# Moving the matmul operands of a gated feed-forward kernel by multiples of 64 bytes in SBUF

## The chip, the cores and the metric

The kernel runs on one core of a Trainium2 chip. The metric is the device time of one execution in microseconds (us); the profile is of one execution and shows each engine: PE is TensorE's matmuls, PEld its weight loads, DVE is VectorE, ACT ScalarE, POOL GpSimd, SP the queue that issues the transfers.

## What is computed

A linear recurrence over 768 time steps with complex decay runs for 4 x 8 heads of width 48, and its output, seen as 3,072 tokens of width 384, goes through a gated feed-forward layer of width 1,536:

```python
new_re = ar * S_re - ai * S_im
new_im = ar * S_im + ai * S_re
S_re, S_im = (new_re + kv, new_im)
y[:, :, t] = np.einsum('bhd,bhde->bhe', q[:, :, t], S_re)
...
g = x @ w_gate
silu = g * (1.0 / (1.0 + np.exp(-g)))
val = x @ w_val
return (silu * val @ w_out).astype(np.float32)
```

## The kernel before

The recurrence is computed in chunks of 128 time steps. A chunk of one batch entry, all 8 heads, is a slab; there are 24. Its decays come from cumulative sums (two matmuls over the triangle `tri`, 384 columns wide, at L504) and functions on ScalarE; its scores and its output from small matmuls (L692, L758). Two slabs make a group g of 256 tokens, 12 groups in all.

The feed-forward layer runs per group in 12 steps of f, 128 of the 1,536 hidden columns each. `f1` (L941) multiplies the group's input, 256 tokens, with gate and value weights of that f: 2 x 3 blocks of 128 rows. For accuracy a number is split into a high and a low part (`xh`, `xl` for the input, `hh`, `hl` for the gated result, two halves of each weight tile), and a product is made of three matmuls: high with high, low with high, high with low. So f1 is 18 matmuls that load 128 columns of a `ww` tile and stream 256 columns of `xh` or `xl`. ScalarE and VectorE then make `sg`, `hh` and `hl`. `f2` (L980) is 9 matmuls that load 128 columns of a `wo` tile and stream 256 columns of `hh` or `hl`. In group 11 f2 is turned round (L974): it loads 128 columns of `hh` or `hl` and streams 384 columns of `wo`, six matmuls in each f step. Group 0 isn't split and runs in plain float32 while the weights arrive.

The order of all work on the engines is worked out ahead by a planner from costs and due times; f1 and f2 of consecutive steps, and the slabs' matmuls of later groups, are interleaved on TensorE by it.

Where a tile lies: `quick` opens the pool `const` and then the pool `work`. Every tile of `work` has a size per partition that is a multiple of 512 bytes: a `ww` tile has 6,144 bytes (`place("w", ...)`), a `wo` tile 3,072, a stage tile 3,072, and each `xh`, `xl`, `hh` and `hl` has its own size plus `TURN_OVER`, 128 numbers or 512 bytes. So all tiles of `work` begin at one address modulo 512. Called 0 here, it is that of both kinds of weights. Inside their larger tiles, x (`xh`, `xl`) begins `INPUT` and h (`hh`, `hl`) begins `GATED` numbers later, both 48, which is 192 bytes:

```python
ahead = GATED if tag in ("hh", "hl") else INPUT
t = work.tile([P, n + TURN_OVER], dt, name=tag, tag=tag, bufs=slots[tag])[:, ahead:ahead + n]
```

`tri` is the first tile of `const`; the sizes behind it add up so that it begins at 384. The blocks of 128 or 256 columns that one matmul reads are multiples of 512 bytes apart, so every read of a tile begins at its tile's offset. The last weight tiles (f = 9 to 11) are lent as buffers to the first stage and later hold the source of the gathers into `T` (L659).

Of the kernel before, what the change touches and what calls it, by code (L numbers as in the profile page):

```python
# [9 lines left out]
F32 = mybir.dt.float32  # L10
# [9 lines left out]
P = 128  # L20
# [37 lines left out]
WIDE_KEYS = 64  # L58
TURNS = P // WIDE_KEYS

TURN_OVER, GATED, INPUT = 128, 48, 48
HIGH, LOW, WHOLE = 0, 1, 2
SHY = -9.7365
POOL_FROM = 9.8301
# [169 lines left out]
def quick(ctx, tc, q, k, v, a_re, a_im, w_gate, w_val, w_out, out, count):  # L234

    nc = tc.nc
    PS = bass.MemoryType.PSUM
    const = ctx.enter_context(tc.tile_pool(name="const", bufs=1))
    work = ctx.enter_context(tc.tile_pool(name="work", bufs=1))
    dram = ctx.enter_context(tc.tile_pool(name="dram", bufs=4, space=bass.MemoryType.DRAM))  # L240
    psum = ctx.enter_context(tc.tile_pool(name="psum", bufs=1, space=PS))
# [16 lines left out]
    G = const.tile([96, B, H, 64], F32, name="G")  # L258
    vts = [const.tile([P, H, 64], F32, name=f"vt{i}") for i in range(2)]
    turned_v = [const.tile([P, 2, 2, 64], F32, name=f"vr{i}") for i in range(2)]  # L260
    W, HALVES = {}, {}
    WIDE = {"w": 2 * DM, "o": DM}

    def place(nm, f, dtype):
        return work.tile([P, 2 * WIDE[nm]], dtype, name=f"w{nm}{f}", tag=f"w{nm}{f}", bufs=1)

    def spare(nm):

        if nm not in W:
            W.pop((nm, NF - 1, WHOLE))  # L270
            W[nm] = place(nm, NF - 1, F32)
        return W[nm]
# [35 lines left out]
    for t, (nm, f, i) in {"re": ("w", 0, 0), "im": ("w", 0, 1), "s1": ("o", 0, 0), "s2": ("w", 1, 0), "s3": ("w", 1, 1),  # L308
                          "qt": ("o", 1, 0), "kt": ("o", 2, 0), "qs": ("w", 2, 0)}.items():
        n, nm_f = 96 if t == "qs" else D, (nm, NF - 3 + f)  # L310
        if nm_f not in W:
            W[nm_f] = place(*nm_f, F32)
        at = W[nm_f][:, i * A2:i * A2 + 2 * H * n].rearrange("p (h d) -> p h d", d=n)
        for j in range(2):
            fixed["lent", t, j] = at[:, H * j:H * j + H], nm_f
# [498 lines left out]
    def weight_ops(f):  # L814
        for nm, n, user in (("w", 2 * DM, "f1"), ("o", DM, "f2")):
# [5 lines left out]
            for i, w in enumerate((w_out,) if nm == "o" else (w_gate, w_val)):  # L821
                def ld(e, i=i, w=w, raw=raw, nm=nm):
                    if i == 0:
                        W.pop((nm, f), None)
                        W[nm, f, WHOLE] = place(nm, f, U32)
                        raw["all"] = W[nm, f, WHOLE].rearrange("p (n t) -> p n t", t=2)
                        raw["low"], raw["high"] = (raw["all"][:, :, x] for x in range(2))
                    o = raw["all"]
                    o = o if nm == "o" else o[:, i * DM:i * DM + DM].rearrange("p (k n) t -> p k n t", k=KT)
                    nc.sync.dma_start(out=o, in_=words(w, nm, f))  # L830
                loads.append(pl.add(f"wl{i}{N}", {"SP": 0.55}, ld, alloc=[] if i else lent, deps=list(loads), lat=1.4, move=1.09))
# [380 lines left out]
@with_exitstack  # L1212
def tile_kernel(ctx, tc, q, k, v, a_re, a_im, w_gate, w_val, w_out, out):
    nc = tc.nc
    w_gate, w_val, w_out = (w if w.dtype == U32 else w.bitcast(U32) for w in (w_gate, w_val, w_out))
    keep = ctx.enter_context(tc.tile_pool(name="keep", bufs=1))

    count = keep.tile([1, 32], I32, name="count")[:, 0:1]
    quick(tc, q, k, v, a_re, a_im, w_gate, w_val, w_out, out, count)
    fit = nc.values_load(count, min_val=0, max_val=P)  # L1220
    with tc.If(fit < P):
        general(tc, q, k, v, a_re, a_im, w_gate, w_val, w_out, out)
# [30 lines left out]
```

## Time and profile before

| | |
|---|---|
| time, median of 3 runs | 639.09 us (635.09 to 642.51) |
| the profiled execution | 636.64 us, its span 634.9 us |
| TensorE busy | 599.6 us, 94% of the span |
| VectorE, ScalarE busy | 504.4 us, 403.5 us |
| matmuls, weight loads | 7,050 each |

The span runs from the first to the last instruction of the profiled execution. A matmul's duration in the profile is longer than the time from its start to the next one's, since matmuls are pipelined; how fast TensorE goes is read from the starts.

### The profile page before, as it was taken

Reading aid. Unit: us, or ns where it says so; the run is one execution under the profiler, and the core shown is the slowest. Engines: PE = TensorE matmul, PEld = TensorE weight load, DVE = VectorE, ACT = ScalarE, POOL = GpSimd, SP = SyncE. Lnnn points to the kernel's source line nnn. Section 1 sums busy time; section 2 is a strip of 40 time slices with the busy share of each in tenths; the row PEclk is TensorE's granted clock in tenths of the full one; section 3 lists DMA queues with packets and bytes.
Section 4 is the critical chain, followed back from the end, with each engine's and each line's share of the span. In section 5 each row is a group of like instructions: output and inputs, shape, how many; then the busy total and the mean of one; then the engine's idle time right before and its main releaser. Section 6 shows DMA issues by size and latency. Waiting matters only on the chain.

```text
span 634.9 us, 17155 instructions
## 1 busy us (share of the span) xinstructions
PE 599.6 (94%) x7050; PEld 564.9 (89%) x7050; DVE 504.4 (79%) x932; ACT 403.5 (64%) x653; POOL 4.2 (1%) x15
## 2 busy tenths in 40 slices
PE   2689999989999999999989999999999999999995
PEld 1477778979989999999989999999999999999995
DVE  8999999999988968878969868769879868544432
ACT  7854548886695785957876975956966863211210
POOL 2000000000000000000000000000000000000000
PEclk9999999999999999999999999999999999999998
DMA  8899701244644654565466464554564642441200
GB/s 256 229 278 270 255 26 38 58 125 117 137 128 116 159 130 105 131 139 133 106 130 154 101 151 115 130 139 112 141 140 124 152 106 62 114 97 51 51 1 29
DMA packets 164218, 79.96 MB, mean 126 GB/s; under 512 B 127387, under 2 KB 159901, under 8 KB 164134
## 3 DMA queue, kind: packets, MB, share of 16 engines
q1 hardware_dynamic: 164134, 78.80, 48.7%
q8 instruction: 57, 0.93, 0.7%
q14 instruction: 27, 0.22, 0.1%
HBM read 59.83 MB, written 4.78 MB: 102 GB/s over the span
## 4 chain that ended last, share of the span: by engine, by line
PE 65%; DVE 13%; DMA 7%; ACT 6%; SPq 4%; issue 3%; DVEq 0%; ACTq 0%
PE p_gv L941 34%; PE p_po L980 13%; PE p_py L692 5%; PE p_ps L692 4%; ACT L1084 4%; PE p_po L974 3%; SPq L659 2%; PE p_pm L504 2%; PE p_pm L758 2%; DMA wo<-in_moe_w_val_dram 2%; DMA re<-in_a_re_dram 2%; ACT s L408 1%; DMA ww<-in_moe_w_val_dram 1%; DVE sg L952 1%; DMA T<-ww 1%
## 5 line engine op out<-in xcount | busy, mean ns | idle before, releaser
L941 PE MATMUL p_gv<-xh,ww 128*128 128x256 f32 x1596 | 305.2, 289 | 5.4 <-DVE sg L952 4.5
L941 PEld LDWEIGHTS p_gv<-xh,ww 128*128 128x128 f32 x1596 | 256.5, 189 | 14.0 <-DVE sg L952 6.7
L941 PE MATMUL p_gv<-xl,ww 128*128 128x256 f32 x726 | 201.6, 278 | 0.0
L1084 ACT ACT_TABLE_LOAD x119 | 152.7, 1283 | 2.1
L941 PEld LDWEIGHTS p_gv<-xl,ww 128*128 128x128 f32 x726 | 136.5, 188 | 0.1
L947 ACT ACTIVATE sg<-p_gv 128x256 f32<-128x256 f32 x144 | 54.6, 384 | 118.2 <-PE p_gv L941 112.9
L980 PE MATMUL p_po<-hh,wo 128*128 128x256 f32 x660 | 119.8, 279 | 0.0
L980 PEld LDWEIGHTS p_po<-hh,wo 128*128 128x128 f32 x660 | 100.7, 188 | 1.8 <-issue 1.8
L952 DVE TENSOR_TENSOR sg<-sg,p_gv 128x256 f32<-128x256 f32 x144 | 58.7, 412 | 52.6 <-ACT sg L947 52.5
L980 PE MATMUL p_po<-hl,wo 128*128 128x256 f32 x330 | 91.7, 278 | 0.0
L980 PEld LDWEIGHTS p_po<-hl,wo 128*128 128x128 f32 x330 | 62.2, 188 | 0.0
L353 DVE TENSOR_TENSOR hl<-sg,hh 128x256 fp32r<-128x256 f32 x132 | 54.6, 417 | 4.9 <-ACT hh L357 0.4
L408 ACT ACTIVATE s<-s 128x768 f32<-128x768 f32 x44 | 36.8, 844 | 12.5 <-DMA fr<-s 6.5
L692 PEld LDWEIGHTS p_ps<-T 96*64 96x64 f32 x768 | 35.8, 138 | 4.1 <-ACT T L357 1.2
L692 PE MATMUL p_ps<-T 96*64 96x128 f32 (+1 forms) x768 | 39.4, 254 | 0.0
L720 DVE TENSOR_TENSOR sc<-p_ps,turn 128x512 f32<-128x512 f32 x48 | 32.2, 687 | 5.2 <-PE p_ps L692 4.9
L357 ACT CAST hh<-sg 128x256 fp32r<-128x256 f32 x51 | 20.3, 402 | 22.7 <-DVE sg L952 15.5
L778 ACT CAST xh<-p_py 128x384 fp32r<-128x384 f32 x22 | 10.6, 480 | 31.0 <-PE p_py L692 30.9
L892 DVE TENSOR_REDUCE flags<-wo 128x1 f32<-128x384 f32 x36 | 19.6, 544 | 11.9 <-DMA wo<-in_moe_w_val_dram 8.6
L897 ACT ACTIVATE wo<-wo 128x384 f32<-128x384 f32 x36 | 19.9, 554 | 12.9 <-DMA wo<-in_moe_w_val_dram 11.6
L359 DVE CAST hh<-sg 128x256 fp32r<-128x256 f32 x81 | 23.1, 290 | 5.7 <-PE p_po L980 2.3
L692 PE MATMUL p_py<-sc,vr 128*32 128x128 f32 x384 | 26.1, 273 | 0.0
(149 smaller groups left out, 895.2 us busy)
## 6 DMA issues: line engine op xcount, KB each, us to landing
T<-ww SPq DMA_DIRECT2D x216, 64.0 KB, 2.5
wo<-in_moe_w_out_dram SPq DMA_DIRECT2D x24, 384.0 KB, 6.0
ww<-in_moe_w_gate_dram SPq DMA_DIRECT2D x12, 384.0 KB
ww<-in_moe_w_val_dram SPq DMA_DIRECT2D x12, 384.0 KB, 6.7
vt<-in_v_dram SPq DMA_DIRECT2D x24, 192.0 KB, 3.2
wo<-in_moe_w_gate_dram SPq DMA_DIRECT2D x12, 384.0 KB, 3.7
wo<-in_moe_w_val_dram SPq DMA_DIRECT2D x12, 384.0 KB, 4.2
re<-in_a_re_dram SPq DMA_DIRECT2D x11, 384.0 KB
```

The source lines that it names most:

```text
L353: V[e].tensor_tensor(out=out, in0=a, in1=b, op=op)
L357: nc.scalar.copy(out=out, in_=in_)
L359: nc.vector.tensor_copy(out=out, in_=in_)
L408: nc.scalar.activation(out=of(dst), in_=of(source), func=func, scale=scale, **kw)
L692: nc.tensor.matmul(out=o, lhsT=l, rhs=r, start=opens, stop=closes, tile_position=(0, width * slot), skip_group_check=True)
L720: nc.vector.tensor_tensor(out=s.rearrange("p (r m) t -> p r m t", m=2), in0=scores[qd].rearrange("p (r m) t -> p r m t", m=2), in1=m, op=A ...
L897: nc.scalar.activation(out=high(0), in_=high(1), func=AF.Square, accum_out=flags[:, fl_hi + j:fl_hi + j + 1])
L941: nc.tensor.matmul(out=gv[:, i, :], lhsT=l, rhs=r, start=(m == 0), stop=(m == len(mm) - 1))
L947: nc.scalar.activation(out=new("sg", I), in_=at_["gv", I][:, 0:2 * P], func=AF.Silu)
L952: nc.vector.tensor_tensor(out=sg, in0=sg, in1=at_["gv", I][:, 2 * P:4 * P], op=ALU.mult)
L980: nc.tensor.matmul(out=po[:, 2 * P * k:2 * P * k + 2 * P], lhsT=l[:, k, :], rhs=r, start=f == 0 and j == 0 and k != 1, stop=f == NF - 1 an ...
L1084: nc.scalar.preload_act_table_set(op.load)
```

## The change

Three offsets change, and the gate and value weights get a pool of their own between `const` and `work`. That pool begins with an empty tile of `STILL`, 112 numbers or 448 bytes; a third pool closes it with 64 empty bytes, so that `work` again begins at the address modulo 512 that it had. Modulo 512 and behind the output weights `wo` at 0, the weights `ww` then lie at 448 (before: 0), x at 128 (before: 192) and h at 64 (before: 192).

```diff
-TURN_OVER, GATED, INPUT = 128, 48, 48
+TURN_OVER, STILL, GATED, INPUT = 128, 112, 16, 32
@@
     const = ctx.enter_context(tc.tile_pool(name="const", bufs=1))
+    still = ctx.enter_context(tc.tile_pool(name="still", bufs=1))
+    gap = ctx.enter_context(tc.tile_pool(name="gap", bufs=1))
     work = ctx.enter_context(tc.tile_pool(name="work", bufs=1))
@@
+    still.tile([P, STILL], F32, name="ahead")
+    gap.tile([P, TURN_OVER - STILL], F32, name="behind")
@@
     def place(nm, f, dtype):
-        return work.tile([P, 2 * WIDE[nm]], dtype, name=f"w{nm}{f}", tag=f"w{nm}{f}", bufs=1)
+
+        pool = still if nm == "w" else work
+        return pool.tile([P, 2 * WIDE[nm]], dtype, name=f"w{nm}{f}", tag=f"w{nm}{f}", bufs=1)
```

## Rows read from the trace of the kernel before

**Rows 1.** The page, parts 1 and 2: engines' busy us, granted clock in 40 slices
```profile
PE 599.6 (94%) x7050; PEld 564.9 (89%) x7050; DVE 504.4 (79%) x932; ACT 403.5 (64%) x653; POOL 4.2 (1%) x15
...
PEclk9999999999999999999999999999999999999998
```

**Rows 2.** The page, part 4: chain that ended last, by engine, by line
```profile
PE 65%; DVE 13%; DMA 7%; ACT 6%; SPq 4%; issue 3%; DVEq 0%; ACTq 0%
PE p_gv L941 34%; PE p_po L980 13%; PE p_py L692 5%; PE p_ps L692 4%; ACT L1084 4%; PE p_po L974 3%; SPq L659 2%; PE p_pm L504 2%; PE p_pm L758 2%; DMA wo<-in_moe_w_val_dram 2%; DMA re<-in_a_re_dram 2%; ACT s L408 1%; DMA ww<-in_moe_w_val_dram 1%; DVE sg L952 1%; DMA T<-ww 1%
```

**Rows 3.** TensorE's waits, 250 to 625 us: engine, line, releaser: total, times, longest
```profile
PE p_pm L504 <- DVE G L353: 1.9, 1, 1.9
PE p_gv L941 <- DVE sg L952: 1.1, 1, 1.1
```

**Rows 4.** Timeline, TensorE from 253.98 us: start, us, engine, line, operation, operands, count
```profile
253.98 0.28 PE L941 MATMUL p_gv<-xl,ww 128*128 128x256 f32 x1
253.98 0.30 PEld L941 LDWEIGHTS p_gv<-xh,ww 128*128 128x128 f32 x2
```

**Rows 5.** Timeline of matmuls: first and last start of one stretch
```profile
253.30 0.28 PE L941 MATMUL p_gv<-xl,ww 128*128 128x256 f32 x1
...
276.42 0.28 PE L941 MATMUL p_gv<-xl,ww 128*128 128x256 f32 x1
```

**Rows 6.** Sums of two windows: length, matmuls' busy us and count, clock, DMA share, GB/s
```profile
253.30:276.50 23.20, 23.20 (x206) 1.00 0.49 116
530.00:553.20 23.20, 23.20 (x200) 1.00 0.40 93
```

**Rows 7.** Timeline of matmuls: first and last start of the other stretch
```profile
530.08 0.28 PE L941 MATMUL p_gv<-xl,ww 128*128 128x256 f32 x1
...
553.17 0.40 PE L941 MATMUL p_gv<-xh,ww 128*128 128x256 f32 x2
```

**Rows 8.** By line, six stretches between 217 and 625 us: count, busy us, mean ns
```profile
L941 PE MATMUL p_gv<-xl,ww 128*128 128x256 f32 x24 | 6.7, 281 | 0.0
L941 PE MATMUL p_gv<-xl,ww 128*128 128x256 f32 x6 | 1.7, 281 | 0.0
L941 PE MATMUL p_gv<-xl,ww 128*128 128x256 f32 x18 | 5.1, 281 | 0.0
L941 PE MATMUL p_gv<-xl,ww 128*128 128x256 f32 x12 | 3.4, 281 | 0.0
L941 PE MATMUL p_gv<-xl,ww 128*128 128x256 f32 x126 | 35.4, 281 | 0.0
L941 PE MATMUL p_gv<-xl,ww 128*128 128x256 f32 x55 | 15.5, 281 | 0.0
```

**Rows 9.** The same by line: 230 to 321 us, and the page's whole span
```profile
L941 PE MATMUL p_gv<-xl,ww 128*128 128x256 f32 x126 | 34.8, 276 | 0.0
...
L941 PE MATMUL p_gv<-xl,ww 128*128 128x256 f32 x726 | 201.6, 278 | 0.0
```

**Rows 10.** Timeline: first of two sums over tri, and the matmul behind them
```profile
285.08 0.34 PE L504 MATMUL p_pm<-s,tri 128*128 128x384 f32 x1
...
285.43 0.28 PE L941 MATMUL p_gv<-xh,ww 128*128 128x256 f32 x1
```

**Rows 11.** Timeline, group 11: fourth and last wide matmul of f2, and the next
```profile
596.33 0.34 PE L974 MATMUL p_po<-wo-1_336,hl 128*128 128x384 f32 x1
...
596.85 0.34 PE L974 MATMUL p_po<-wo-1_336,hl 128*128 128x384 f32 x1
597.03 0.28 PE L941 MATMUL p_gv<-xh,ww 128*128 128x256 f32 x1
```

**Rows 12.** Tile T and its gathers, 250 to 625 us: who waited for it: us, times
```profile
  DVE ww L650: 2.5, 3
  DVE sc L720: 2.3, 2
  DVE G L353: 1.6, 3
```

## Prediction

> **What bounds the kernel now.** I read the page first. TensorE is the bound: it shows 599.6 us busy in a span of 634.9 us, at the full granted clock until the last slice, so at its 2.4 GHz level throughout [rows 1]. The chain that ended last is 65% TensorE, and its two largest lines are L941 (the matmuls into p_gv, "f1") and L980 (those into p_po, "f2") [rows 2]. Then the waits: from 250 to 625 us TensorE waits 3.0 us in all for another engine [rows 3]. There the time is a count of matmuls times their step, the time from the start of one to the start of the next, and a change in the step reaches the end undiminished.
>
> The count follows from the loops. Groups 1 to 11 run 12 steps of f of 18 matmuls in f1, 11 x 12 x 18 = 2,376. Groups 1 to 10 run 9 in f2, 10 x 12 x 9 = 1,080. Together there are 3,456 matmuls that stream 256 columns, each with a load of 128 columns. The load for the next one runs beside the stream of the present one: the load issued at 253.98 lies under the matmul of 253.98 [rows 4]. So at every moment two reads of SBUF are under way, and their addresses are what the change moves.
>
> Now the step. In one undisturbed stretch 206 matmuls show in a window of 23.20 us [rows 6]; one of them began before 253.30, so 205 start between 253.30 and 276.42 [rows 5], 204 steps in 23.12 us: 113.3 ns. In another stretch of the same length 200 show [rows 6]; three began before it, so 197 start between 530.08 and 553.17 [rows 7], 196 steps in 23.09 us: 117.8 ns. The same instructions, shapes and distances run at two levels, which I call the short and the long step. They differ by 4.45 ns. The mean duration of a matmul tells them apart too, 281 ns in a long stretch [rows 8] and 276 ns in a short one [rows 9].
>
> How much runs long: by the matmuls that read xl, the long stretches hold 24 + 6 + 18 + 12 + 126 + 55 = 241 [rows 8] of 726 [rows 9], a third. A third of 3,456 is about 1,150 matmuls, and 1,150 x 4.45 ns = 5.1 us are paid now for the long step. Everything else, some 2,310 matmuls, runs short.
>
> **The change part by part.** It removes and adds no instruction, no transfer and no wait; the order is the same. It adds two tiles that nobody touches. What moves is where tiles begin, modulo 512 bytes. Call distance the start of the streamed tile minus that of the tile loaded beside it, modulo 512. Before, x and h lie at 192 and both kinds of weights at 0, so all 27 pairs of an f step have distance 192. After:
> - f1 with f1 (17 pairs of 27): 128 - 448 = 192 modulo 512, as before.
> - the last of f1 with the first load of f2 (1 pair): 128 - 0 = 128.
> - f2 with f2 (8 pairs): 64 - 0 = 64.
> - the last of f2 with the first load of f1 (1 pair): 64 - 448 = 128.
>
> So nothing moves within f1; f2 and the two seams do.
>
> What the distance is worth, the trace shows only on 384-wide matmuls. At distance 320 (group 11 streams wo and loads hh) three steps take 0.52 us, 173 ns each, and the seam behind them at distance 0 takes 0.18 us [rows 11]. Two steps at 128 and 0 (the sums over tri) take 0.35 us, 175 ns each [rows 10]. At the short step's rate per column 384 columns would take 170 ns. So the rows give 3 to 10 ns of stall for a wide matmul at other distances. That is the bound from above for f2 at 64: up to 10 ns on 1,080 matmuls, 10.8 us, less the 1.6 us that f2's third of long steps costs already, so +9.2 us. The bound from below is the short step everywhere in f2, 1,080 x 0.33 x 4.45 ns = 1.6 us gained; below that nothing, since no row has a shorter step than 113 ns. I take the row with most repeats, 320: 173.3 x 256/384 = 115.5 ns, 2.2 ns over the short step, 2.4 us on 1,080 matmuls.
>
> What it does to f1 is the larger half. The long step is a lasting pattern: it starts at a restart of TensorE and runs to the next one, over whole groups (126 xl matmuls of one stretch) [rows 8]. With one distance for all 27 pairs nothing on the way disturbs it. After the change each f step passes through 10 pairs at 64 and 128, so the two reads meet in another phase four times in 3.1 us. I expect that the long pattern doesn't hold through that and f1 falls back to the short step, which is the commoner one. That takes off the 5.1 us.
>
> **A rule that speaks against it.** These rows show steps that differ by distance and by stretch, with TensorE waiting for nobody [rows 3, 10, 11]. The Trainium skill, "TensorE: Matmul & The Clock Gate", Part 2, says that TensorE has two independent SBUF read ports and that loading the next weights takes no read bandwidth from the running matmul. By that rule addresses can't matter and the sum would be 636.6 us, unchanged; the two levels of one loop in the trace don't agree with it, though they don't prove that addresses are the cause.
>
> The rest is small. Group 11's 72 wide matmuls go from 320 to 448; with a stall of 0 to 10 ns in place of today's 3 that is -0.2 to +0.5 us. The 42 sums over tri meet other distances, a few ns each, under 0.3 us. The gate weights' tiles are also where the gathers into T start; from 250 to 625 us only VectorE waited for them, 6.4 us in all, and TensorE never [rows 12], so 64 bytes more or less there cost nothing as long as that holds. ScalarE and VectorE write x and h at other offsets, with the same sizes; where they wait on TensorE, that is hidden.
>
> Sum, on the profiled execution's own time: 636.64 - 5.1 + 2.4 = 633.9, call it 634. That execution stands 2.5 us under the median of 639.09; the three runs spread over 7.4 us, which is what 1,670 matmuls passing from one step to the other would make, so part of that spread may be the share of long steps.
>
> **The rivals.**
> 1. Nothing changes: the share of long steps is drawn at each restart as now. For it: 55 xl matmuls in the last stretch keep the long step although every f step there has six wide matmuls at another distance between them [rows 8, 11]. Against it: the wide rows differ by distance. Time 636.6, between 635 and 642.5 as the runs shown. Chance 0.30.
> 2. The other side: the pairs at 64 and 128 push every step into the long pattern. For it: the wide seam at distance 0 stalls most [rows 11] and the last 120 us are long already. Against it: after the sums over tri, at 128 and 0, the short step comes back [rows 9, 10]. Price 2,310 x 4.45 ns = 10.3 us, 646.9. It decides by itself once 9 matmuls of 10 run long. Chance 0.17.
> 3. f2 alone pays the upper bound, with f1 as now: 636.64 + 9.2 = 645.8. From 114.8 ns on f2's step outweighs what it saves, and at 123 ns the kernel is 1% slower. For it: 64 lies between 0 and 128, the distances of the worse rows. Chance 0.11.
>
> **How the numbers follow.** The forecast, f1 short throughout and f2 between 113.3 and 117.8 ns, has 0.42 and its own range is 631.5 (636.64 - 5.1) to 636.3 (f2 all long, + 4.8). The range that holds 8 in 10 takes in rival 1 and the lower parts of 2 and 3: 630 to 646. One per cent, about what a measurement here can tell from no change, is 632.7 and 645.5 about the median. Below 632.7 lies somewhat more than half of the forecast's chance, counting in a step shorter than any row has: 0.25. Above 645.5 lie most of rival 2 and half of rival 3: 0.20. The rest is 0.55.
>
> **What would show it.** Right: xl matmuls last 276 ns in the mean from 505 to 625 us too, and 205 starts fit in 23.1 us there; f2's step is near 115. Rival 1: stretches of 281 and 276 ns still alternate. Rival 2: 281 ns everywhere. Rival 3: f2's step near 123 ns with f1 mixed. A step below 113 ns anywhere would make my lower bound wrong.

## The result: slower by 0.6%, with the forecast's main step reversed

| | before | after |
|---|---|---|
| time, median of 19 runs each | 638.29 us (635.09 to 642.51) | 642.12 us (639.11 to 645.98) |
| ratio after to before | | 1.0061, 95% interval 1.0044 to 1.0078 |
| the profiled execution, its span | 636.64 us, 634.9 us | 640.98 us, 639.2 us |

The time lies inside the range of 630 to 646 and within 1% of before, but it moved the other way: 3.8 us up between the medians, where the forecast had 2.6 us down from the profiled execution.

The page after, of which I show TensorE's and the other engines' busy us (part 1), the granted clock (part 2), the chain of waits (part 4) and four groups of matmuls (part 5: count, busy us, mean ns):

```profile
PE 606.2 (95%) x7050; PEld 573.0 (90%) x7050; DVE 504.6 (79%) x932; ACT 404.1 (63%) x653; POOL 4.2 (1%) x15
...
PEclk9689999999999999999999999999999999999998
...
PE 75%; DVE 11%; DMA 4%; ACT 4%; SPq 4%; issue 2%; DVEq 0%
...
L947 PE MATMUL p_gv<-xh,ww 128*128 128x256 f32 x1596 | 310.0, 291 | 6.1 <-ACT xh L784 3.3
...
L947 PE MATMUL p_gv<-xl,ww 128*128 128x256 f32 x726 | 202.9, 279 | 0.0
...
L986 PE MATMUL p_po<-hh,wo 128*128 128x256 f32 x660 | 122.2, 281 | 0.0
...
L986 PE MATMUL p_po<-hl,wo 128*128 128x256 f32 x330 | 92.1, 279 | 0.0
```

Lines are 6 higher than before: L947 is f1, L986 is f2, L980 the turned f2 of group 11. Against [rows 1, 2] the counts are the same to the instruction, VectorE and ScalarE are the same within 0.6 us, and TensorE has 6.6 us more in its matmuls (8.1 us in its weight loads, which run beside them). Its share of the chain rose from 65 to 75%. The xl matmuls' mean went from 278 ns [rows 9] to 279.

TensorE's waits from 250 to 625 us, as [rows 3] (total, times, longest):

```profile
PE p_pm L510 <- DVE G L359: 0.5, 1, 0.5
PE p_gv L947 <- DVE sg L958: 0.2, 1, 0.2
```

The same two waits, 0.7 us in place of 3.0. Over all from 100 us on, the waits sum to 5.7 us after and 9.3 before. I read this as a slower TensorE that reaches VectorE's results later and waits less for them; then of what TensorE lost, 3.6 us came back at its own waits.

**Where the time went.** I sort the steps of 256-wide matmuls from 100 us on by the pair they pass through (start to start, breaks left out), and give the mean. These means, like the counts of stretches further down, are of one profiled execution of each kernel. xx is f1, hh is f2, xh the seam into f2, hx the seam back into f1:

| pair | distance before, after | recorded steps after | ns before | ns after | difference |
|---|---|---|---|---|---|
| xx | 192, 192 | 2,230 | 114.81 | 116.48 | +3.7 us |
| hh | 192, 64 | 951 | 114.61 | 117.68 | +2.9 us |
| xh | 192, 128 | 91 | 114.67 | 120.01 | +0.5 us |
| hx | 192, 128 | 80 | 114.81 | 115.91 | +0.1 us |

Some 7.2 us more on TensorE, 3.6 us of it back at the waits; beside that f1 of group 1 starts 1.7 us later (102.6 against 100.9 us), in a profile whose granted clock shows 6 and 8 tenths in its second and third slice, so partly the 1.2 GHz level, after a first slice with TensorE 2 tenths busy (before's first slice is as idle, and its clock did not fall). These terms give 5.3 us for the 4.3 us between the spans; the 1.0 us left I have not followed. The early clock is not what sets the two kernels apart: the granted clock averaged 0.992 over the 19 runs of after, and 0.992 over the 62 runs of before that stand beside the experiments below.

The largest term is the one that I had with the other sign: f1, whose own distance did not move. The timeline of matmuls (start us, duration, line, operands, count) shows it happen behind a restart:

```profile
256.30 0.28 PE L947 MATMUL p_gv<-xl,ww 128*128 128x256 f32 x1
...
257.32 0.28 PE L947 MATMUL p_gv<-xl,ww 128*128 128x256 f32 x1
257.44 0.28 PE L947 MATMUL p_gv<-xh,ww 128*128 128x256 f32 x1
257.56 0.40 PE L986 MATMUL p_po<-hh,wo 128*128 128x256 f32 x2
257.79 0.28 PE L986 MATMUL p_po<-hl,wo 128*128 128x256 f32 x1
...
258.50 0.28 PE L986 MATMUL p_po<-hl,wo 128*128 128x256 f32 x1
258.61 0.28 PE L947 MATMUL p_gv<-xh,ww-1_292 128*128 128x256 f32 x1
258.73 0.28 PE L947 MATMUL p_gv<-xl,ww-1_292 128*128 128x256 f32 x1
...
260.50 0.28 PE L947 MATMUL p_gv<-xl,ww-1_292 128*128 128x256 f32 x1
```

Every third matmul reads xl. Before the first f2 there are 9 steps in 257.32 - 256.30 = 1.02 us, 113.3 ns: short. In f2 6 steps take 0.71 us, 118 ns. And in the next f1, the same instructions at the same distance, 15 steps take 1.77 us, 118.0 ns: long. A window of 23.20 us from the restart on holds 199 matmuls, near the 200 of the long window of before and not the 206 of the short one (columns as in [rows 6]):

```profile
255.60:278.80 23.20, 23.20 (x199) 1.00 0.47 116
```

To count this over the whole trace I call a stretch a row of 256-wide matmuls of one line without a break, and long when the steps of its second half average 115 ns or more. Behind a restart means behind a break or behind other matmuls, the sums over tri and group 11's wide f2 among them:

| stretch | before: long of all | after: long of all |
|---|---|---|
| f1 behind a restart | 16 of 51 | 17 of 49 |
| f1 behind f2 | 27 of 78 | 72 of 80 |
| f2 behind f1 | 28 of 89 | 91 of 91 |

A restart gives f1 what it gave it before. The way through f2 and back turns it long.

### The profile page after: what moved, and what is told of

Its sections match the earlier page's. It is cut to its first block, busy times and chain, and to the rows that moved or that the text cites. A ratio compares the mean times of both kernels' runs of the same rounds, so it can differ in the third digit from the quotient of the medians.

```text
span 639.2 us, 17155 instructions
## 1 busy us (share of the span) xinstructions
PE 606.2 (95%) x7050; PEld 573.0 (90%) x7050; DVE 504.6 (79%) x932; ACT 404.1 (63%) x653; POOL 4.2 (1%) x15
## 4 chain that ended last, share of the span: by engine, by line
PE 75%; DVE 11%; DMA 4%; ACT 4%; SPq 4%; issue 2%; DVEq 0%
PE p_gv L947 39%; PE p_po L986 16%; PE p_py L698 5%; PE p_ps L698 5%; PE p_po L980 4%; SPq L665 2%; PE p_pm L510 2%; PE p_pm L764 2%; ACT L1090 1%; DMA wo<-in_moe_w_val_dram 1%; DMA T<-ww 1%; ACT s L414 1%; DMA dr<-qs 1%; DVE ww L359 1%; PE p_gv L636 1%
## 5 line engine op out<-in xcount | busy, mean ns | idle before, releaser
L947 PE MATMUL p_gv<-xh,ww 128*128 128x256 f32 x1596 | 310.0, 291 | 6.1 <-ACT xh L784 3.3
L947 PEld LDWEIGHTS p_gv<-xh,ww 128*128 128x128 f32 x1596 | 259.1, 190 | 14.7 <-DVE sg L958 4.4
L947 PE MATMUL p_gv<-xl,ww 128*128 128x256 f32 x726 | 202.9, 279 | 0.0
L947 PEld LDWEIGHTS p_gv<-xl,ww 128*128 128x128 f32 x726 | 136.5, 188 | 0.1
L986 PE MATMUL p_po<-hh,wo 128*128 128x256 f32 x660 | 122.2, 281 | 0.0
L986 PEld LDWEIGHTS p_po<-hh,wo 128*128 128x128 f32 x660 | 101.6, 188 | 1.8 <-issue 1.8
L986 PE MATMUL p_po<-hl,wo 128*128 128x256 f32 x330 | 92.1, 279 | 0.0
L986 PEld LDWEIGHTS p_po<-hl,wo 128*128 128x128 f32 x330 | 62.0, 188 | 0.0
```

Of the source, the lines that this page charges most:

```text
L947: nc.tensor.matmul(out=gv[:, i, :], lhsT=l, rhs=r, start=(m == 0), stop=(m == len(mm) - 1))
L986: nc.tensor.matmul(out=po[:, 2 * P * k:2 * P * k + 2 * P], lhsT=l[:, k, :], rhs=r, start=f == 0 and j == 0 and k != 1, stop=f == NF - 1 an ...
```

## The experiments

### The bare stream: step against distance

The slab work and all data flow are left out and zeros are written: only blocks of 36 matmuls that load 128 and stream 256 columns at one distance, with a break of TensorE between blocks (four blocks a distance), then a run of 128 f steps with the distances of four layouts.

```diff
+UNIFORM = [0, 32, 64, 96, 128, 160, 192, 224, 256, 288, 320, 352, 384, 416, 448, 480]
+PATTERNS = [(0, 0, 192, 192), (448, 0, 128, 64), (0, 0, 192, 64), (448, 0, 128, 192)]
```

> A bare stream that leaves the whole computation out and writes zeros: 36 matmuls of the kernel's form (load 128 columns, stream 256, fp32r) per block, one distance between streamed and loaded tile per block, 16 distances in steps of 32 bytes, 4 blocks each after a short idle; then 8 f steps of 18 and 9 matmuls with the four address sets before, after, f2 alone, seams alone. Theory pair (each pair costs what its own distance costs): distance 192 gives steps of 113.3 or 117.8 ns, 64 gives 117.7 or more in every block, 128 gives 118 to 120, 0 the most; in the pattern of after the 17 pairs of f1 stay at 113.3 or 117.8 as the restart drew them. Theory phase (a step depends on what the pairs before it did to the alignment of the two reads): the uniform blocks look alike at every distance, two levels each, and only patterns that change the distance on the way are long throughout. In both, the pattern of after averages about 116.9 ns, that of before between 113.3 and 117.8.

Measured, as the mean step from the 13th of a block on:

| distance | ns | distance | ns |
|---|---|---|---|
| 0, 256 | 120.0 | 128, 384 | 118.5 to 120.0 |
| 32, 288 | 116.5 to 117.8 | 160, 416 | 117.2 to 118.5 |
| 64, 320 | 117.7 to 117.8 | 192, 448 | 113.3 in three blocks, 117.7 to 117.8 in the fourth |
| 96, 352 | 119.8 to 120.1 | 224, 480 | 118.1 to 118.4 |

The step depends on the distance, in a stream without any other work, and repeats with 256 bytes, not 512. At 192 it has two values, the short and the long step of the kernel; at 64 all eight blocks (64 and 320) show the long one, 117.7 to 117.8. So f2 at 64 does not need the passage through other distances to be long. The run of f steps began long, and at the layout of before it stayed so, as its timeline shows (every f step 362.84 - 359.66 = 3.18 us, by 27 matmuls 117.8 ns):

```profile
359.66 2.28 PE L47 MATMUL gv<-px,pw 128*128 128x256 f32 x18
361.78 1.22 PE L54 MATMUL po<-ph,pv 128*128 128x256 f32 x9
362.84 2.28 PE L47 MATMUL gv<-px,pw 128*128 128x256 f32 x18
```

In the part with the layout of after, f1 had 117.60, f2 117.75, the seams 120.91 and 116.06 ns, near the 116.48, 117.68, 120.01 and 115.91 of the kernel. Its first f1 started short, and from the second on, behind f2 at 64 and the seam at 128, all were long (18 matmuls in 2.22 us, then in 2.28):

```profile
458.24 2.22 PE L47 MATMUL gv<-px,pw 128*128 128x256 f32 x18
460.31 1.22 PE L54 MATMUL po<-ph,pv 128*128 128x256 f32 x9
461.37 2.28 PE L47 MATMUL gv<-px,pw 128*128 128x256 f32 x18
```

With the layout of f2 alone f1 had 117.53 and f2 118.12 ns; with that of the seams alone f1 went back to the short step within each f step (114.42 in the mean) and f2 had 117.37. Neither theory holds whole: blocks of one distance differ by their distance, as the first said, and a pair on the way changes the stretch behind it, as the second said.

### f2 alone at 64

```diff
-TURN_OVER, GATED, INPUT = 128, 48, 48
+TURN_OVER, GATED, INPUT = 128, 16, 48
```

The kernel before with h alone moved: f1 at 192, seam into f2 at 192, f2 at 64, seam back at 64.

> Only the gated tiles move, from 192 to 64: f1 at 192, f1 to f2 at 192, f2 at 64, f2 to f1 at 64. Theory pair: f2's 1,080 steps go to 117.7 ns as in after (+3.1 ns, +3.3 us), f1 keeps its mean of 114.8; ratio 1.004 to 1.006. Theory phase: f1's mean rises as well, to 116 to 117 ns, +6 to +8 us on TensorE and a ratio of 1.006 to 1.010.

Measured: 638.74 us, ratio 1.0018 (0.999 to 1.0046). hh 117.80, xx 115.57, mean of all 116.25 ns; f1 behind f2 is long in 36 of 79 stretches. By line:

```profile
L941 PE MATMUL p_gv<-xl,ww 128*128 128x256 f32 x726 | 202.2, 279 | 0.0
L980 PE MATMUL p_po<-hh,wo 128*128 128x256 f32 x660 | 122.5, 281 | 0.0
```

f2 costs what it costs after (122.5 against 122.2 us of hh), f1 only a part: its mean lies between what the two theories expected, 114.8 and 116 to 117. f2 at 64 by itself moves the time by an amount that these runs do not tell from zero, less than either theory expected.

### The seams alone

```diff
-TURN_OVER, STILL, GATED, INPUT = 128, 112, 16, 32
+TURN_OVER, STILL, GATED, INPUT = 128, 112, 48, 32
```

The changed kernel with h put back to 192: f1 and f2 at 192, the seam into f2 at 128, the seam back at 192 - 448 = 256 modulo 512.

> Only the two seams move: f1 at 192, f1 to f2 at 128, f2 at 192, f2 to f1 at 256. Theory pair: the 131 seams f1 to f2 cost 120 ns as in after (+5 ns, +0.7 us), f1 and f2 keep means of 114.8 and 114.6; ratio 1.000 to 1.002. Theory phase: two disturbances in each f step make f1 and f2 long in most steps, means of 116 to 117.8; ratio 1.004 to 1.012.

Measured: 641.46 us, ratio 1.005 (1.0027 to 1.0073). xx 115.50, hh 116.83, xh 118.03, hx 116.99 ns. One pair of 27 at 128 and one at 256, and f2, whose own distance is that of before, is long in 89 of 89 stretches behind f1. f1 behind f2, entered through 256, is long in 17 of 79. f2's mean is as the phase theory had it, f1's is not. So a single pair can decide for the stretch behind it, and which way depends on its distance.

### All pairs at 64

```diff
-TURN_OVER, GATED, INPUT = 128, 48, 48
+TURN_OVER, GATED, INPUT = 128, 16, 16
```

> The kernel before with both input and gated tiles at 64 bytes, one distance of 64 for all 27 pairs. Theory map (uniform distance 64 gave 117.8 ns in all 8 blocks of the bare stream): every f1 and f2 step is 117.8 ns, no 113 anywhere, 3 to 4 us more TensorE time per execution than before's mixture of about 115 in the mean (3,456 x 2.8 ns = 9.7 us), partly taken back by fewer waits in the first 250 us; ratio 1.008 to 1.014. Theory phase (only changes of distance on the way do harm, one distance is as good as another): the mixture of 113.3 and 117.8 of before; ratio 0.997 to 1.003.

Measured: 642.65 us beside 637.34, ratio 1.0077 (1.0049 to 1.0105). xx 117.34, hh 117.25, mean 117.34 ns, 2.59 over before: 2.59 x 3,456 = 9.0 us on TensorE for some 5 us of time. The waits from 100 us on are 6.7 us, 2.6 less than before; they account for a part of the difference, and the rest I have not followed. f1 is long behind a restart too, in 47 of 49 stretches. But 64 has the short pattern as well: from 258 to 285 us every f step ran short, and of the stretches behind one another 16 of 171 are short. Two matmuls at the same place of neighbouring f steps stand 263.79 - 260.73 = 3.06 us apart there, by 27 matmuls 113.3 ns:

```profile
260.73 0.28 PE L980 MATMUL p_po<-hl,wo 128*128 128x256 f32 x1
...
263.79 0.28 PE L980 MATMUL p_po<-hl,wo 128*128 128x256 f32 x1
```

So the bare stream's eight long blocks had not shown all that 64 can do, and the expected "no 113 anywhere" does not hold. With 117.34 ns this is the price of rival 2 nearly in full, and it comes to half of what I had put on it.

### The seams exchanged

Which of the two turns f1 long in the changed kernel, the f2 at 64 or the seam at 128 behind it? Here f2 is at 192, the seam into f2 at 256 and the seam back into f1 at 128.

```diff
-TURN_OVER, STILL, GATED, INPUT = 128, 112, 16, 32
+TURN_OVER, STILL, GATED, INPUT = 128, 16, 48, 64
```

> The changed kernel with other offsets: gate weights at 64, x at 256, h at 192, output weights at 0. f1 has distance 192 and f2 has distance 192, as before the change; the seam from f1 into f2 is at 256 and the seam from f2 into f1 at 128. So the two seams of the run with both seams moved change places: there the seam into f2 was at 128 and all 89 stretches of f2 behind f1 were long, while of 79 stretches of f1 behind f2, entered through 256, only 17 were. In the changed kernel 72 of 80 stretches of f1 behind f2 are long; their entry is at 128, but f2 at 64 lies before them too. Theory (the pattern of a stretch at 192 is set by the distance of the seam through which it is entered; 128 gives the long one): of about 80 stretches of f1 behind f2 at least 65 long, of about 90 stretches of f2 behind f1 at most 45 long; mean steps about 116.5 to 117.5 ns in f1 and 114 to 115.5 in f2; time 640 to 645 us beside 638.5. Rival (it is the f2 at 64, not the seam, that puts f1 into the long pattern): of the stretches of f1 behind f2 at most 35 long, mean step of f1 near 115.5, time within 3 us of before.

Measured: 640.75 us beside 637.94, ratio 1.0037 (1.0006 to 1.0068). f1 behind f2 is long in 81 of 81 stretches, f2 behind f1 in 17 of 90. The two lines have changed places against the run before. The timeline shows one f step in the middle of a long run, f1 behind f2, then f2, then the next f1:

```profile
320.04 0.28 PE L947 MATMUL p_gv<-xl,ww 128*128 128x256 f32 x1
...
321.80 0.28 PE L947 MATMUL p_gv<-xl,ww 128*128 128x256 f32 x1
321.92 0.28 PE L947 MATMUL p_gv<-xh,ww 128*128 128x256 f32 x1
322.04 0.40 PE L986 MATMUL p_po<-hh,wo 128*128 128x256 f32 x2
322.28 0.28 PE L986 MATMUL p_po<-hl,wo 128*128 128x256 f32 x1
...
322.96 0.28 PE L986 MATMUL p_po<-hl,wo 128*128 128x256 f32 x1
...
323.19 0.28 PE L947 MATMUL p_gv<-xl,ww 128*128 128x256 f32 x1
...
324.96 0.28 PE L947 MATMUL p_gv<-xl,ww 128*128 128x256 f32 x1
```

f1 runs long, 15 steps in 1.76 and again in 1.77 us; f2 between them takes 0.24 us for its first two steps and then 6 steps in 0.68 us, 113.3 ns. In these f steps the seam at 256 leads from the long pattern into the short one and the seam at 128 out of it again. Behind a short f1 the seam at 256 does the opposite, as the first f step behind a restart shows: 15 steps of f1 in 261.12 - 259.42 = 1.70 us, 113.3 ns, then 6 steps of f2 in 0.71 us, 118 ns:

```profile
259.42 0.28 PE L947 MATMUL p_gv<-xl,ww 128*128 128x256 f32 x1
...
261.12 0.28 PE L947 MATMUL p_gv<-xl,ww 128*128 128x256 f32 x1
...
261.59 0.28 PE L986 MATMUL p_po<-hl,wo 128*128 128x256 f32 x1
...
262.30 0.28 PE L986 MATMUL p_po<-hl,wo 128*128 128x256 f32 x1
```

The forecast for the mean of f1, 116.5 to 117.5 ns, holds (116.78); that of f2 is missed by a little (116.03 for 114 to 115.5), since the stretches right behind a restart came out long in 14 of 28.

Put together, for stretches at distance 192 by the distance of the seam through which they are entered, and by the stretch that lies before the seam:

| entered through | kernel | line | long of all | long behind a long one | long behind a short one |
|---|---|---|---|---|---|
| 192 | before | f2; f1 | 28 of 89; 27 of 78 | 28 of 28; 27 of 27 | 0 of 61; 0 of 51 |
| 256 | seams alone; exchanged | f1; f2 | 17 of 79; 17 of 90 | 2 of 64; 0 of 73 | 15 of 15; 17 of 17 |
| 64, behind f2 at 64 | f2 alone | f1 | 36 of 79 | 35 of 78 | 1 of 1 |
| 128 | seams alone; exchanged | f2; f1 | 89 of 89; 81 of 81 | 19 of 19; 18 of 18 | 70 of 70; 63 of 63 |
| 128, behind f2 at 64 | after | f1 | 72 of 80 | 71 of 79 | 1 of 1 |

So a seam at 192 keeps the pattern, in 167 of 167 stretches; a seam at 256 changes it for the other one, in 167 of 169; a seam at 128 puts the stretch behind it into the long one, whatever went before.

### A finer map, and a layout without the choice

The bare stream again (the computation left out as above), with distances 4 bytes apart between 160 and 224, six blocks each, some others, and 192 made from two other pairs of addresses.

```diff
+UNIFORM = [(0, 160), (0, 164), ..., (0, 112), ..., (64, 256), (448, 128)]
```

> The bare stream again (all other work left out, zeros written), 6 blocks of 36 matmuls for each distance: 160 to 224 in steps of 4 bytes, single values elsewhere, and distance 192 made in two other ways (loaded tile at 64 and streamed at 256; 448 and 128). Theory map (the step is a function of the distance modulo 256, with a narrow place near 192 where 113.3 ns is possible): neighbours of 192 within a line of the memory also show 113.3 ns, some of them perhaps in all 6 blocks; from 176 down and 208 up the step is 116 to 119; 64 against 256 and 448 against 128 look like 192, both levels. Rival (where the tiles lie counts, not the distance): these two differ from 192 and show 117 or more in every block.

Measured: within 4 bytes of 192 the step goes to 117.7 (188) and 121.1 ns (196); 192 made as 256 - 64 and as 128 - 448 behaves as 192 (short in 6 of 6 and 5 of 6 blocks; here the difference counts and not the addresses). That refutes the rival; the theory's short neighbours of 192 are not there either. One other distance is short, 112, and there in all six blocks. The timeline gives a row for each block (start, duration of all 36, operands): three of the six at 192, two of the six at 112, one at 200:

```profile
281.57 4.37 PE L47 MATMUL gv<-x192by0at,w0at 128*128 128x256 f32 x36 [0.56 <-DVE gv L59]
286.51 4.51 PE L47 MATMUL gv<-x192by0at,w0at 128*128 128x256 f32 x36 [0.58 <-DVE gv L59]
291.62 4.37 PE L47 MATMUL gv<-x192by0at,w0at 128*128 128x256 f32 x36 [0.60 <-DVE gv L59]
...
343.96 4.60 PE L47 MATMUL gv<-x200by0at,w0at 128*128 128x256 f32 x36 [0.76 <-DVE gv L59]
...
718.19 4.36 PE L47 MATMUL gv<-x112by0at,w0at 128*128 128x256 f32 x36 [0.80 <-DVE gv L59]
723.36 4.40 PE L47 MATMUL gv<-x112by0at,w0at 128*128 128x256 f32 x36 [0.81 <-DVE gv L59]
```

4.37 us is a short block at 192 and 4.51 a long one; at 112 a block can take 4.40, since it starts slower, but every one ends at 113.3.

The rest of the multiples of 4:

> The computation is left out, zeros are written; the bare stream again (36 matmuls that load 128 and stream 256 columns, three blocks per distance), at the 36 distances in steps of 4 between 4 and 252 that are not yet measured, and 112 and 368 once more. If the step repeats with 256 bytes, 112 and 368 show 113.3 ns in all blocks. Theory: the shortest step seen, 113.3 ns, is a floor that few distances reach; of the new ones between 0 and 6 do, the others lie at 115 to 124 ns. Rival: a distance below 113.3 exists, down to the 107 ns at which 256 columns would pass at one per cycle of 2.4 GHz; then the kernel before was never at the floor.

Measured: 112 and 368, which is 112 + 256, show 113.3 ns in three of three blocks each. The other 35 distances lie at 117.7 to 124.6 ns. With the runs above all 64 multiples of 4 below 256 are measured: 112 always short, 192 short in 22 of 26 blocks (448 among them), no other below 116.5, none below 113.3 (three blocks or more of the bare stream at each).

And the kernel before with everything at 112:

```diff
-TURN_OVER, GATED, INPUT = 128, 48, 48
+TURN_OVER, GATED, INPUT = 128, 28, 28
```

> The kernel before with x and h both 112 bytes behind the weights modulo 512 instead of 192, so all 27 pairs of an f step have distance 112; nothing else differs. In the finer map of the bare stream, distance 112 showed a step of 113.3 ns in all six of its blocks, while 192 showed 113.3 in five and 117.8 in one. Theory (the step is set by the distance, and the share of long steps in the kernel before comes from 192 having two patterns of which one is long): every f step short, mean step about 113.4 ns in place of 114.75, 1.35 ns x 3456 = 4.7 us less on TensorE; as in the changed kernel part of it is taken up by waits elsewhere, so the time is 1 to 4.5 us below that of before. Rival (the long step is drawn at a restart of TensorE whatever the distance, as in rival 1 of the prediction): a mixture as before, mean step 114 to 115.5 ns, time within 1 us. Second rival (in the kernel other reads of SBUF disturb the stream and what the bare stream shows does not carry over): steps of 116 to 120 ns, time 3 to 10 us above.

Measured: 636.48 us (12 runs) beside 638.39 (17 runs), ratio 0.9972 (0.9945 to 0.9998). It is the fastest of the kernels here, by 1.9 us against before. Its busy engines, a xl group of the page, and a window in each of the two places of [rows 6]:

```profile
PE 598.5 (94%) x7050; PEld 564.1 (89%) x7050; DVE 504.5 (80%) x932; ACT 404.0 (64%) x653; POOL 4.2 (1%) x15
...
L941 PE MATMUL p_gv<-xl,ww 128*128 128x256 f32 x726 | 200.5, 276 | 0.0
```

```profile
253.80:277.00 23.20, 23.20 (x205) 1.00 0.48 114
529.90:553.10 23.20, 23.20 (x207) 1.00 0.39 93
```

Both windows hold about the count of the short step now, 205 and 207 for 206 and 200. Of the f1 and f2 stretches that follow each other 0 of 167 are long. What remains is the start: behind a restart mostly 5 to 11 steps run at 115 to 121 ns before the short step is there, and with some 80 restarts the mean is 114.35, 0.40 ns under before, 1.4 us on TensorE. The expected 113.4 had left that start out; the time came out inside the 1 to 4.5 us, at its lower end. A part of the 1.9 us can be the granted clock: it averaged 0.993 in these runs and 0.991 in before's beside them, by the slope given further down an estimated 0.5 us.

All kernels beside each other (ns are means over all 256-wide steps; us is the difference to before times 3,456):

| kernel | ns | us on TensorE | waits from 100 us on | ratio (interval) |
|---|---|---|---|---|
| all at 112 | 114.35 | -1.4 | 8.7 us | 0.9972 (0.9945 to 0.9998) |
| before | 114.75 | 0 | 9.3 us | 1 |
| seams alone | 115.98 | +4.3 | 7.8 us | 1.0050 (1.0027 to 1.0073) |
| f2 alone at 64 | 116.25 | +5.2 | 6.5 us | 1.0018 (0.999 to 1.0046) |
| seams exchanged | 116.61 | +6.4 | 7.4 us | 1.0037 (1.0006 to 1.0068) |
| after | 116.90 | +7.4 | 5.7 us | 1.0061 (1.0044 to 1.0078) |
| all at 64 | 117.34 | +9.0 | 6.7 us | 1.0077 (1.0049 to 1.0105) |

The times follow the mean step, but not strictly. Of what TensorE loses about half arrives in after and in all at 64, a fifth in f2 alone, three quarters in the seams alone. The last two stand in the other order than their steps, with intervals that overlap. Their runs also had unlike granted clocks, 0.994 and 0.989 in the mean, which by the slope given further down makes an estimated 1.3 of the 2.0 us between them; beyond that I did not settle it.

## Why the prediction failed, by its own steps

**What moves.** Right: the counts and the order are the same, and the step of the 256-wide matmuls is where the time moved. That addresses set the step, which the trace of before could not prove, the bare stream shows. The rule that was weighed against it, the two independent SBUF read ports of the Trainium skill, "TensorE: Matmul & The Clock Gate", Part 2, read as addresses can't matter, does not agree with these runs: the same stream takes 113.3 to 124.6 ns a step by the distance alone, and 636.6 us by that reading became 641.0 in the profiled execution.

**f1 falls back to the short step, -5.1 us.** Wrong, and this is the step that failed. From rows of a kernel with one distance throughout I argued that passing through other distances breaks up the long pattern and leaves the commoner one. The passage does act on the pattern, but the result is not the commoner one: the seam's distance settles it. Behind 128 a stretch at 192 is long in 170 of 170 cases where its line and the other were both at 192; behind 256 it is the opposite of the stretch before it in 167 of 169. In after the way back into f1 is at 128, so f1 went from a third long to 72 of 80 behind f2, and the term is +3.7 us. Why the 8 others stayed short, with f2 at 64 before them, is open. Only the first f1 behind a restart kept its old odds, 17 long of 49.

**f2 at 64 costs 2.2 ns over the short step, 2.4 us.** Right in sign, too small. hh stands at 117.68 in after, 4.4 ns over 113.3, twice the 2.2; against before's mixture it is +3.1 ns, some 3.3 us on 1,080. I had scaled the 384-wide step of 173 ns at distance 320 down by columns to 115.5 ns; the bare stream at 320 shows 117.7 to 117.8 in its four blocks. The stall at 320 is no smaller for the narrower matmul, 4.4 ns over 113.3 where the wide one had 3.3 over 170. The upper bound of 10 ns held.

**A change in the step reaches the end undiminished.** Wrong for a loss. I read the 3.0 us of waits [rows 3] as too few to matter, and left out that they sink when TensorE gets slower: 3.0 to 0.7 us in that window, 9.3 to 5.7 from 100 us on. About half of what TensorE lost did not reach the end, in after and in all at 64; in after the waits account for it, in all at 64 only for 2.6 us of some 4.

**Rival 2, all long, 646.9.** The nearest mechanism, at chance 0.17: about 80% of after's steps, some 2,670 of 3,352, are in long runs, for some 1,060 of 3,343 before (by a moving average of the step). It stopped short of its price because f1 behind a restart is short two times in three, and because of the waits. The evidence that I had against it, the short step coming back behind the sums over tri [rows 10], was misread: before those sums the step was short too. The long stretch of 126 xl matmuls [rows 8] has sums over tri inside it, and goes on long behind them:

```profile
513.57 0.33 PE L504 MATMUL p_pm<-s,tri 128*128 128x384 f32 x1
```

Of the 35 such places of before's trace where the step can be read on both sides it is the same in 32, long in 3 of them. Pairs at other distances had not brought back the short step there. And the one place of before's trace with other pairs inside every f step, group 11, had stayed long [rows 8, 11]; I gave that to rival 1. In after, group 11's f1 is short, long, long in turn, behind seams of 173, 169 and 176 ns.

**Rival 3, f2 alone pays.** f2 paid its 2.9 us, far under the 9.2; alone it moved the time by 0.2%, not told from zero.

**The small terms** held: VectorE's waits for T go from 6.4 [rows 12] to 6.5 us, group 11's wide steps from 174.3 to 176.2 ns in the mean of 60, 0.1 us.

**The spread of the runs.** I put part of before's 7.4 us of spread down to the share of long steps. The runs' granted clocks give another part: over 62 runs of before the mean clock went from 0.981 to 0.999, and a straight line through them gives 2.4 us less for 0.01 more, so some 4.4 us from end to end. It leaves a scatter of 1.5 us (one standard deviation), and the share of long steps was read in one execution alone, so what that share adds to the spread is not shown.

## What to carry to other kernels

Where a matmul engine is the bound and nobody waits, count starts in a window and turn it into a step per matmul: two stretches of the same code with different steps are a question worth asking, and the answer can be where operands begin in SBUF. Price such a move by a bare stream at the exact width and distance, over many restarts (eight blocks at 64 missed its short pattern), and don't scale it from another width. When a layout has more than one distance, the pair at a seam counts, however rare, since it can decide what the whole stretch behind it does; one distance for all pairs that showed nothing but the short step once it ran (112 here) came out ahead of one that is usually short (192), by 0.3% with an interval that just leaves out zero.

## What the runs showed of the hardware that was not expected

- The step of a 128-column load beside a 256-column stream depends on the distance of their addresses modulo 256, at full granted clock, in the bare stream: 113.3 ns at 112, 117.8 at 64, 120.0 at 0, up to 124.6 at others. A move by 4 bytes, 192 to 196, costs 7.8 ns a matmul.
- At 192 the same stream has two lasting patterns, 113.3 and 117.8 ns. A pair at 192 keeps the pattern (167 of 167 stretches), one pair at 128 makes the next stretch long (170 of 170), one pair at 256 changes it for the other pattern (167 of 169). At 64 the kernel ran short for 27 us on end and mostly long elsewhere. What in the chip makes the pattern, these runs don't show.
- No block of the bare stream ran under 113.3 ns, at any of the 64 multiples of 4 bytes below 256.
